# Expert rows sorted in DRAM, loaded by plain DMAs and turned on VectorE instead of TensorE

## Chip, cores and metric

The kernel runs on one core of a Trainium2 chip. The metric is device time in microseconds (us); lower is better.

## The reference, cut to what matters

```python
# x (8 batches, 8 heads, 512, 64), state (8, 8, 32, 64)
a  = softmax(scale * x @ state.T);  xread = a @ state        # 512 rows a batch
a2 = softmax(scale * state @ x.T);  sread = a2 @ x           # 32 rows a batch
x  = concat([xread, sread])                                  # 4608 tokens x 512
h  = x @ w_in                                                # dense layer, 2048 wide
x  = (h * clip(h + 3, 0, 6) / 6) @ w_out
e  = argmax(x @ w_gate)                                      # 8 experts, one for each token
out[mask] = gate_w * eom * (relu(x[mask] @ w1[e]) @ w2[e])   # expert layer, 1024 wide
```

## The kernel before

**Dense part.** Eight batches go through attention and the dense layer, 16 steps (`ft`) each; the last segment (`NB`) holds the 256 `sread` tokens of all batches together. Precision is kept by splitting each float32 operand into a high and a low part (ScalarE makes the high one by a cast, VectorE the low one by a subtraction) and by three matmuls for each product.

**Routing.** When a segment has ended, `routed` copies the layer's output to `x2`, feature by token. `write_rows` turns it into token rows (VectorE transposes of 32x32 blocks, L539) and SyncE (SP) writes these to the DRAM tensor `xd` in pieces of 512 bytes. `logits`, `turn_logits`, `choose`, `ranks` and `place` find each token's expert and its place in that expert's list; `scatter` then writes token number and weight of 128 tokens to the DRAM table `tab` at that place, one indirect DMA on GpSimd (POOL) for each tile of 128 tokens (L642).

**Expert part.** It goes in slots, in the order of `ORDER`. 16 big slots take 256 places of one expert's list each; a pair takes twice 64 places of two experts, and three pairs run here (slots 5, 10 and 18 counted from 0). For a slot `gather` reads 128 ids and weights for each half from `tab` (L868) and then the rows named there from `xd` (L874), all on POOL. `turn` then makes them feature by token: four 128x128 TensorE transposes for each 128 rows into PSUM (L889), an evacuation by ScalarE that is also the high part (L893, or L896 for a pair), and the low part from PSUM on VectorE (L894). In a big slot `gemm1` (L937, 12 matmuls a step) and `gemm2e` (L953, L956, L957, six a step, one step behind) run over 8 steps; each step needs two splits of weights (L932 and L933, L942 and L943) and one of `h` (L946, L947). `finish` scales the result and scatters it to `out` on POOL (L971). The turn of slot s+1 stands in step 4 of slot s.

**What sets the order.** The work is listed in program order, and a scheduler places each engine's instructions; every engine and every DMA queue then takes its own in order. SP issues the loads of weights (L861), two buffers of 4.2 MB for the big slots and two for the pairs, the weights of an expert being loaded only if its buffer does not hold them already. The places of the first nine big slots come from `lists1`, made in step 5 of the last dense segment; those of the rest from `lists2`, in slot 1, when the 256 `sread` tokens are placed too. The tile tag `xr` has two buffers, for `write_rows`, for the first gathered rows and for `y`; the tag `x2T` has one, for `x2` and for the scratch of the lists.

Of the kernel before, what the change touches and what calls it, by code (L numbers as in the profile page):

```python
# [19 lines left out]
DM, DF = 512, 2048  # L20
# [3 lines left out]
CAP = NT  # L24
# [22 lines left out]
def cat_consts():  # L47
# [17 lines left out]
    parts["part"] = p  # L65
    parts["high"] = p >= 64
    parts["part64"] = p % 64 + TR
# [13 lines left out]
def tile_kernel(  # L81
# [36 lines left out]
    flat = tab.rearrange("a (b o) -> (a b) o", o=2)  # L118
# [385 lines left out]
    placed = []  # L504
# [9 lines left out]
    def routed(po, n, tile0, part=None):  # L514
# [4 lines left out]
        if n == 512:  # L519
            x2.append(mp.tile([128, 2, n], F32, tag="xr", name="x2b", bufs=2) if tile0 == 28 else  # L520
                      ap.tile([128, 2, n], F32, tag="x2b", name="x2b", bufs=1))
        r.x2 = [t[:, k, :] for t in x2 for k in range(1024 // n)]
        r.made = []
# [113 lines left out]

    def scatter(r, behind=()):

        new = []  # L640
        for t in range(r.nt):
            i = G.indirect_dma_start(flat, bass.IndirectOffsetOnAxis(ap=r.dsti[:, t:t + 1], axis=0),  # L642
                                     toku[:, r.tile0 + t, :], None).ins
            for d in behind:
                tc.add_manual_dep(i, d.name, DEP, reason="rows are written first")
            for o in new:
                tc.declare_no_dep(i, o, reason="places are distinct")
            after(i, placed)
            new.append(i)
        placed[:] = new  # L650

    def route(r):
# [5 lines left out]
        if r.n > 256:  # L658
            write_rows(r, 1)
        yield  # L660
# [3 lines left out]
        place(r)  # L664
        scatter(r)
        yield
# [103 lines left out]
    def weights_regs(es, n, tag):  # L770


        regs = one("regs" + tag, 2 * n, mybir.dt.int32)
        V.tensor_copy(regs[:, :n], es)
        V.memset(regs[:, n:n + 2], 1)
        V.tensor_tensor(regs[:, n + 2:], es[:, 2:], es[:, :n - 2], op=ALU.not_equal)
# [3 lines left out]
    def list256(k, n, pos, tag, used):  # L780
# [11 lines left out]
        idu = one("idu" + tag, n, U32)  # L792
        V.tensor_scalar(idu, bases, 0.5, C("part"), op0=ALU.mult, op1=ALU.add)
        return idu, weights_regs(es, n, tag)
# [8 lines left out]
    def lists2():  # L803
# [9 lines left out]
        idm, regm = list256(2 * NE, NM, "posm", "m", took)  # L813
# [18 lines left out]
        b0, b1 = [bases.rearrange("p (j two) -> p two j", two=2)[:, i, :] for i in range(2)]  # L832
        V.tensor_tensor(b1, b1, b0, op=ALU.subtract)
        V.scalar_tensor_tensor(b1, b1, C("high"), b0, op0=ALU.mult, op1=ALU.add)
        idu = one("idu2", NP, U32)
        V.tensor_scalar(idu, b1, C("part64"), None, op0=ALU.add)
        regu = one("regsu", 2 * NU, mybir.dt.int32)
        V.tensor_copy(regu[:, :NU], es2)
        V.tensor_copy(regu[:, NU:], ok)
        used = one("used", 1, mybir.dt.int32)  # L840
        V.tensor_copy(used, total)
        return {"m": (idm, regm), "p": (idu, regu), "used": used}
# [22 lines left out]
    def gather(n, table, idx, rows):  # L865

        ids = cp.tile([128, 4], U32, tag="ids", name="ids", bufs=6)
        i = G.indirect_dma_start(ids[:, :2 * n], None, table, bass.IndirectOffsetOnAxis(ap=idx, axis=0)).ins  # L868
        after(i, placed)
        xg = []  # L870
        both = None if qa else mp.tile([128, 2, DM], F32, tag="xr", name="xg0", bufs=2)
        for t in range(n):
            x = qa["p"].tile([128, DM + 8], F32, tag="xg", name="xg", bufs=4)[:, :DM] if qa else both[:, t, :]
            G.indirect_dma_start(x, None, rows, bass.IndirectOffsetOnAxis(ap=ids[:, 2 * t:2 * t + 1], axis=0))  # L874
            xg.append(x)
        return ids, xg

    def turn(xg):

        n = len(xg)  # L880
        if n == 2:
# [461 lines left out]
```

## Time and profile before

| | |
|---|---|
| device time, median of 3 runs | 1118.22 us (1117.49 to 1118.74) |
| profiled execution, its own device time | 1119.56 us |
| its span, first to last instruction | 1117.8 us |
| granted TensorE clock, mean | 0.997 |
| TensorE busy | 1087.9 us |
| VectorE / ScalarE / GpSimd busy | 699.5 / 556.8 / 126.2 us |
| DMA moved | 128.47 MB |

The span is that of the one profiled execution; its device time is 1.76 us more than its span and 1.34 us above the median of the runs. The dense part lasts from the start to about 688 us of the span, the expert part from there to the end. A row of the chain of work gives the time from the start, the length and what it is; a row of the lines gives count, busy time and mean of one.

### The profile page before, as it was taken

The page shows a single profiled execution, that of the slowest core. Times are in us where ns is not written, and L with a number is a line of the kernel's source. Part 1 is how long each engine was busy: PE and PEld are TensorE (multiplying, and loading weights), DVE is VectorE, ACT ScalarE, POOL GpSimd, SP SyncE. Part 2 cuts the span into 40 slices and gives each one's busy share as a digit, 9 for nine tenths or more (in the row PEclk, how much of TensorE's full clock was granted, in tenths as well). Part 3 has the DMA queues.
Part 4 walks back from the last instruction along what each step waited for, and adds up shares of the span by engine and source line. Part 5 has one row for each costly group of instructions (what it writes and reads, how often), then busy time and mean ns, then how long its engine had stood idle before and what let it go on. Part 6 is the DMA issues. An engine that isn't in the chain of part 4 may idle for free.

```text
span 1117.8 us, 18409 instructions
## 1 busy us (share of the span) xinstructions
PE 1087.9 (97%) x6904; PEld 863.0 (77%) x6904; DVE 699.5 (63%) x1456; ACT 556.8 (50%) x1061; POOL 126.2 (11%) x137
## 2 busy tenths in 40 slices
PE   4899999999999999999999999999999999999997
PEld 2557776777777777777777899999869987999994
DVE  7997867755746747556555476966446645666651
ACT  4768834433434434334343345666545644666551
POOL 0000000110010010100100122331122122121101
PEclk9999999999999999999999999999999999999999
DMA  7647140411202103110010048195195769812300
GB/s 230 208 120 260 48 113 19 135 41 38 76 3 72 45 1 77 41 28 13 1 38 1 1 113 304 53 341 192 49 312 176 246 208 332 320 58 96 142 19 30
DMA packets 55007, 128.47 MB, mean 115 GB/s; under 512 B 7280, under 2 KB 25968, under 8 KB 54896
## 3 DMA queue, kind: packets, MB, share of 16 engines
q1 hardware_dynamic: 47616, 108.80, 29.8%
q0 software_dynamic: 7296, 18.43, 4.8%
q8 instruction: 56, 0.92, 0.4%
q14 instruction: 39, 0.32, 0.1%
HBM read 137.13 MB, written 19.71 MB: 140 GB/s over the span
## 4 chain that ended last, share of the span: by engine, by line
PE 93%; DVE 3%; DMA 1%; issue 1%; ACT 1%; POOL 0%; POOLq 0%; SPq 0%; DVEq 0%; ACTq 0%
PE h L460 16%; PE h L937 16%; PE o L499 11%; PE o L500 11%; PE o L501 11%; PE o L953 5%; PE o L957 5%; PE o L956 5%; PE misc L227 3%; PE h L474 2%; PE h L904 1%; PE misc L889 1%; PE o L923 1%; PE misc L553 1%; PE misc L391 1%
## 5 line engine op out<-in xcount | busy, mean ns | idle before, releaser
L500 PE MATMUL o<-gh,wo 128*128 128x512 f32 x512 | 200.5, 392 | 0.9 <-DVE wo L725 0.9
L499 PE MATMUL o<-gh,wo 128*128 128x512 f32 x512 | 199.3, 393 | 1.7 <-ACT wo L724 1.7
L501 PE MATMUL o<-gl,wo 128*128 128x512 f32 x512 | 199.9, 390 | 0.0
L490 DVE SCALAR_TENSOR_TENSOR g<-r,h 128x512 f32<-128x512 f32 x128 | 87.5, 684 | 121.2 <-ACT r L489 120.6
L489 ACT ACTIVATE r<-h 128x512 f32<-128x512 f32 x128 | 76.7, 599 | 167.6 <-PE h L460 167.5
L943 DVE TENSOR_TENSOR vl<-w2s,vh 128x512 fp32r<-128x512 f32 x128 | 89.2, 698 | 105.7 <-ACT vh L942 99.2
L942 ACT CAST vh<-w2s 128x512 fp32r<-128x512 f32 x128 | 79.3, 620 | 101.3 <-PE o L957 97.8
L491 ACT CAST gh<-g 128x512 fp32r<-128x512 f32 x128 | 79.3, 620 | 76.8 <-DVE g L490 76.0
L499 PEld LDWEIGHTS o<-gh,wo 128*128 128x128 f32 x512 | 95.9, 188 | 28.0 <-issue 4.4
L492 DVE TENSOR_TENSOR gl<-g,gh 128x512 fp32r<-128x512 f32 x128 | 88.3, 690 | 46.2 <-ACT gh L491 44.8
L500 PEld LDWEIGHTS o<-gh,wo 128*128 128x128 f32 x512 | 96.3, 188 | 23.9 <-issue 2.1
L501 PEld LDWEIGHTS o<-gl,wo 128*128 128x128 f32 x512 | 96.3, 188 | 20.4
L460 PE MATMUL h<-ah,sh 128*128 128x512 f32 x256 | 106.7, 418 | 4.3 <-ACT sh L447 2.6
L933 DVE TENSOR_TENSOR wl<-w1s,wh 128x512 fp32r<-128x512 f32 x128 | 88.4, 691 | 30.1 <-ACT wh L932 24.3
L642 POOL DMA_INDIRECT tab<-toku,ldsti x34 | 33.8, 995 | 648.6 <-DVE ldsti L636 414.2
L460 PE MATMUL h<-al,sh 128*128 128x512 f32 x256 | 102.6, 401 | 0.3 <-DVE al L291 0.3
L460 PE MATMUL h<-ah,sl 128*128 128x512 f32 x256 | 101.1, 396 | 0.1
L957 PE MATMUL o<-vh,hl 128*128 128x512 f32 x256 | 100.3, 392 | 0.0
L956 PE MATMUL o<-vl,hh 128*128 128x512 f32 x256 | 100.1, 391 | 0.0
L932 ACT CAST wh<-w1s 128x512 fp32r<-128x512 f32 x128 | 79.5, 622 | 35.5 <-PE h L937 31.5
L937 PEld LDWEIGHTS h<-xh,wh 128*128 128x128 f32 x512 | 76.5, 188 | 11.7 <-issue 2.0
L937 PE MATMUL h<-xh,wh 128*128 128x256 f32 x512 | 82.8, 283 | 0.8 <-ACT xh L893 0.8
(225 smaller groups left out, 1815.6 us busy)
## 6 DMA issues: line engine op xcount, KB each, us to landing
w1s<-w SPq DMA_DIRECT2D x88, 512.0 KB
w2s<-w SPq DMA_DIRECT2D x88, 512.0 KB
xd<-xr SPq DMA_DIRECT2D x68, 128.0 KB
xT<-xT SPq DMA_DIRECT2D x16, 512.0 KB
wi<-w_in SPq DMA_DIRECT2D x16, 512.0 KB
wraw<-w_out SPq DMA_DIRECT2D x16, 512.0 KB
xq<-xq SPq DMA_DIRECT2D x16, 512.0 KB
half<-xp SPq DMA_DIRECT2D x4, 256.0 KB
```

The costliest lines, as they stand in the source:

```text
L460: T.matmul(ps, w[:, o:o + 128], a[:, e, :], start=(n == 0), stop=(n == 5))
L490: V.scalar_tensor_tensor(g6, r, 6.0, ps, op0=ALU.min, op1=ALU.mult)
L492: V.tensor_tensor(gl, g6, gh.bitcast(F32), op=ALU.subtract)
L499: T.matmul(po[k][:, :n], woh[ft][:, s], gh, start=first, stop=False)
L500: T.matmul(po[k][:, :n], wol[ft][:, s], gh, start=False, stop=False)
L501: T.matmul(po[k][:, :n], woh[ft][:, s], gl, start=False, stop=last)
L932: S.copy(wh, a)
L933: V.tensor_tensor(wl, a, wh.bitcast(F32), op=ALU.subtract)
L937: T.matmul(ps, w[:, k, :], x[:, k, :], start=(m == 0), stop=(m == 11))
L943: V.tensor_tensor(vl, c, vh.bitcast(F32), op=ALU.subtract)
L956: T.matmul(py[t], hh[:, sl], vl, start=False, stop=False)
L957: T.matmul(py[t], hl[:, sl], vh, start=False, stop=(ft == 7))
```

## The change

Routing also sorts the rows themselves. A new DRAM tensor `xs` has a place for each place of the lists. `read_rows` reads the rows that `write_rows` has put in `xd` back into SBUF, token by partition, and `sort_rows` scatters them, whole rows of 2 KB, to their places in `xs`, one indirect DMA on POOL for each 128 tokens, two in step 11 of a segment's timetable and two in step 12; the scatter to `tab` moves to step 13 and behind them. After the last 256 tokens `zero_tails` writes 64 rows of zeros behind each expert's last row (four indirect DMAs).

An expert slot then loads its places of `xs` by plain DMAs on SP: `load_rows` reads the first place from a register, issues four pieces (a quarter of the features each, 128 floats of 256 rows, to 32 partitions), and a fifth DMA for ids and weights (`own`, from `tab`). `turn` no longer uses TensorE or PSUM: VectorE turns the pieces in 32x32 blocks, four instructions of 128x256 for a big slot (four of 128x128 for a pair), between SBUF tiles; ScalarE's cast and VectorE's subtraction then read SBUF, in two halves. The pair has no copy left. The lists give bases in place of indices, and `w1` is laid out on the host so that its rows fit the order of the features. `turn(s+1)` and the load for slot s+3 now stand in step 3 of slot s (step 4 of a pair); before, the gather for slot s+2 stood in step 1. In the last step but one of a slot, `hl` may not come ahead of the turned rows.

```diff
-    xd = tc.dram_tile([NT + 128, DM], F32, name="xd")
-    tab = tc.dram_tile([NTAB // 2, 4], U32, name="tab")
+    xd = tc.dram_tile([NT, DM], F32, name="xd")
+    xs = tc.dram_tile([NTAB, DM], F32, name="xs")
+    tab = tc.dram_tile([NTAB, 2], U32, name="tab")
...
+    def read_rows(r, c):
+        nt = min(2, r.nt - 2 * c)
+        r0 = 128 * r.tile0 + 256 * c
+        t = mp.tile([128, 2, DM], F32, tag="xr", name="xt", bufs=2)[:, :nt, :]
+        D.dma_start(t, xd[r0:r0 + 128 * nt, :].rearrange("(t p) n -> p t n", p=128))
+        r.rows.extend(t[:, k, :] for k in range(nt))
+
+    def sort_rows(r, t0, t1, behind=()):
...
+            i = G.indirect_dma_start(xs, bass.IndirectOffsetOnAxis(ap=r.dsti[:, t:t + 1], axis=0), r.rows[t], None).ins
...
     def scatter(r, behind=()):
...
+            tc.add_manual_dep(i, put[-1].name, LATER, reason="rows are wanted first")
...
     def route(r):
...
+        read_rows(r, 0)
+        if r.n > 256:
+            read_rows(r, 1)
         yield
         choose(r)
         ranks(r)
         yield
         place(r)
+        sort_rows(r, 0, r.nt)
         scatter(r)
+        if r.n == 256:
+            zero_tails()
...
-    def gather(n, table, idx, rows):
...
-            G.indirect_dma_start(x, None, rows, bass.IndirectOffsetOnAxis(ap=ids[:, 2 * t:2 * t + 1], axis=0))
+    def load_rows(bases, n):
+        xg = qa["p"].tile([128, 8, 128], F32, tag="xg", name="xg", bufs=2) if qa else \
+            mp.tile([128, 8, 128], F32, tag="xr", name="xg0", bufs=2)
+        own = cp.tile([128, 2, 2], U32, tag="own", name="own", bufs=5)
+        a = n // 32
+        for j, reg in enumerate(bases):
+            base = D.value_load(reg, min_val=0, max_val=NTAB - n)
+            for g in range(4):
+                i = D.dma_start(xg[32 * g:32 * g + 32, a * j:a * j + a, :],
+                                xs[bass.ds(base, n), 128 * g:128 * g + 128].rearrange("(a u) c -> u a c", u=32)).ins
+                after(i, put)
...
-                T.transpose(ps[:, 128 * k:128 * k + 128], xg[t][:, 128 * k:128 * k + 128], ident)
...
-                S.copy(xh[:, :, s], ps3)
-                V.tensor_tensor(xl[:, :, s], ps3, xh[:, :, s].bitcast(F32), op=ALU.subtract)
+        x = mp.tile([128, 4, 256], F32, tag="x2T", name="xt", bufs=1) if got_first else \
+            mp.tile([128, 4, 256], F32, tag="xr", name="xt0", bufs=2)
+        for c in range(2):
+            s = slice(2 * c, 2 * c + 2)
+            for k in range(2 * c, 2 * c + 2):
+                V.transpose(x[:, k, :], V_in[:, :, k, :])
+            S.copy(xh[:, s], x[:, s])
+            i = V.tensor_tensor(xl[:, s], x[:, s], xh[:, s].bitcast(F32), op=ALU.subtract)
...
+        if ft == 6:
+            tc.add_manual_dep(i.ins, last_turned[0].name, LATER, reason="the next rows first")
...
             for t in ws[1][0] + ws[1][1]:
-                G.tensor_copy(t[0:1, 0, 0:1].bitcast(U32), got[0][0][0:1, 0:1])
+                G.tensor_copy(t[0:1, 0, 0:1], got[0][1][0:1, 0, 0:1])
             fetch_weights(1)
-    fetch_rows(1)
...
+    fetch_rows(1)
+    fetch_rows(2)
...
-            if ft == 1 and s + 2 < first:
-                fetch_rows(s + 2)
-            if ft == 4 and s + 1 < first:
-                turned[s + 1] = turn(got[s + 1][1])
+            if ft == 3:
+                turn_next(s)
```

## Rows read from the trace of the kernel before

**Rows 1.** Page: busy time of engines, DMA share in 40 slices of the span.

```profile
PE 1087.9 (97%) x6904; PEld 863.0 (77%) x6904; DVE 699.5 (63%) x1456; ACT 556.8 (50%) x1061; POOL 126.2 (11%) x137
DMA  7647140411202103110010048195195769812300
```

**Rows 2.** Page: the chain that ended last, by line.

```profile
PE h L460 16%; PE h L937 16%; PE o L499 11%; PE o L500 11%; PE o L501 11%; PE o L953 5%; PE o L957 5%; PE o L956 5%; PE misc L227 3%; PE h L474 2%; PE h L904 1%; PE misc L889 1%; PE o L923 1%; PE misc L553 1%; PE misc L391 1%
```

**Rows 3.** Chain in order of time: start, us, what; slots 0 and 1, last pair's turn.

```profile
704.93 1.40 PE h L937 x12
...
727.24 0.87 PE misc L889 x8
728.12 1.42 PE h L937 x12
...
1085.09 0.44 PE misc L889 x4
```

**Rows 4.** Chain in order of time, from the dense part into slot 0.

```profile
688.07 0.14 PE o L501
...
688.23 0.62 ACT wh L932
688.85 0.98 ACT xh L893 x2
...
689.87 0.74 PE h L937 x4
```

**Rows 5.** Lines of TensorE and VectorE: count, busy us, mean ns, idle before.

```profile
L889 PE MATMUL misc<-ident,xg 128*128 128x128 f32 x140 | 18.5, 273 | 0.0
L539 DVE STREAM_TRANSPOSE xr<-x2b 128x256 f32<-128x256 f32 x32 | 11.8, 407 | 0.0
L894 DVE TENSOR_TENSOR xl<-misc,xh 128x512 fp32r<-128x512 f32 x32 | 20.5, 680 | 0.8 <-issue 0.8
L630 DVE TENSOR_TENSOR lpos<-misc,carry 128x8 f32<-128x8 f32 x34 | 5.6, 165 | 1.2
```

**Rows 6.** Windows, slots 0 to 2: us; busy of PE, PEld, DVE, ACT, POOL; clock, DMA, GB/s.

```profile
690.00:713.30 23.30, 23.26 (x160) 20.58 (x161) 21.31 (x81) 13.04 (x28) 5.51 (x5) 1.00 0.14 32
713.30:736.50 23.20, 23.20 (x155) 21.09 (x154) 20.15 (x66) 14.33 (x28) 7.83 (x7) 1.00 0.61 218
736.50:759.70 23.20, 23.20 (x154) 21.10 (x154) 14.82 (x26) 14.24 (x29) 5.38 (x5) 1.00 0.89 343
```

**Rows 7.** Timeline of VectorE at the turn in slot 3.

```profile
774.95 1.28 DVE L894 TENSOR_TENSOR xl<-misc,xh 128x512 fp32r<-128x512 f32 x2
776.15 0.68 DVE L933 TENSOR_TENSOR wl<-w1s,wh 128x512 fp32r<-128x512 f32 x1
```

**Rows 8.** Chain in order of time, the step of slot 3 behind that turn.

```profile
777.25 1.40 PE h L937 x12
```

**Rows 9.** Windows: two bursts of row writes in 512-byte pieces, a stretch of weight loads.

```profile
645.00:648.00 3.00, 3.00 (x27) 2.96 (x27) 2.17 (x6) 1.20 (x4) 0.00 (x0) 1.00 0.85 173
657.00:660.00 3.00, 3.00 (x28) 3.00 (x27) 2.00 (x10) 0.91 (x2) 0.96 (x1) 1.00 0.79 138
672.00:690.00 18.00, 17.19 (x145) 16.95 (x145) 9.82 (x20) 9.48 (x21) 6.58 (x14) 1.00 1.02 402
```

**Rows 10.** Timeline of POOL, scatters to the table.

```profile
654.17 0.96 POOL L642 DMA_INDIRECT tab<-toku,ldsti  x1 [0.30 <-issue]
655.43 1.12 POOL L642 DMA_INDIRECT tab<-toku,ldsti  x1 [0.30 <-issue]
...
703.05 1.41 POOL L642 DMA_INDIRECT tab<-toku,ldsti  x1 [23.10 <-DVE scr L766]
```

**Rows 11.** Timeline of SP's DMA issues, weights of slot 0 and of the first pair.

```profile
663.08 2.11 SPq L861 DMA_DIRECT2D w1s<-w  x4
...
724.15 2.16 SPq L861 DMA_DIRECT2D w1s<-w  x4
```

**Rows 12.** Chain in order of time, landing of rows scattered to `out`.

```profile
1099.16 2.77 DMA out<-y,ids
```

More of the change, by code (lines that the diff above doesn't have):

```diff
@@ L636, in place @@
         V.tensor_copy(r.dsti, dst)
+    def read_rows(r, c):
[5 more added lines that the diff above has]
+    def sort_rows(r, t0, t1, behind=()):
+        if t0 == 0:
+            r.sorted = []
+        for t in range(t0, t1):
+            i = G.indirect_dma_start(xs, bass.IndirectOffsetOnAxis(ap=r.dsti[:, t:t + 1], axis=0), r.rows[t], None).ins
+            for d in behind:
+                tc.add_manual_dep(i, d.name, DEP, reason="in its time")
+            for o in r.sorted:
+                tc.declare_no_dep(i, o, reason="places are distinct")
+            after(i, put)
+            r.sorted.append(i)
+        if t1 == r.nt:
+            put[:] = r.sorted
     def scatter(r, behind=()):
@@ L791, in list256 @@
         V.scalar_tensor_tensor(bases, C(pos), 256.0, bases, op0=ALU.mult, op1=ALU.add)
-        idu = one("idu" + tag, n, U32)
-        V.tensor_scalar(idu, bases, 0.5, C("part"), op0=ALU.mult, op1=ALU.add)
-        return idu, weights_regs(es, n, tag)
+        return weights_regs(es, bases, n, tag)
     def lists1():
@@ L831, in lists2 @@
         V.scalar_tensor_tensor(bases, bases, -float(TR), ok, op0=ALU.add, op1=ALU.mult)
[L832 to L837, printed above, removed]
+        regu = one("regsu", 3 * NU, mybir.dt.int32)
         V.tensor_copy(regu[:, :NU], es2)
-        V.tensor_copy(regu[:, NU:], ok)
+        V.tensor_copy(regu[:, NU:2 * NU], ok)
+        V.tensor_scalar(regu[:, 2 * NU:], bases, float(TR), None, op0=ALU.add)
         used = one("used", 1, mybir.dt.int32)
         V.tensor_copy(used, total)
-        return {"m": (idm, regm), "p": (idu, regu), "used": used}
+        return {"m": regm, "p": regu, "used": used}
     ws = {}
@@ new lines, in zero_tails @@
+    def zero_tails():
+        z = mp.tile([128, DM], F32, tag="xr", name="zeros", bufs=2)
+        G.memset(z, 0.0)
+        pair = carry.rearrange("p (j two) -> p two j", two=2)
+        ends, tails = one("ends", NE // 2), one("tails", NE // 2, U32)
+        V.tensor_tensor(ends, pair[:, 1, :], pair[:, 0, :], op=ALU.subtract)
+        V.scalar_tensor_tensor(ends, ends, C("half"), pair[:, 0, :], op0=ALU.mult, op1=ALU.add)
+        V.tensor_scalar(tails, ends, C("part64"), None, op0=ALU.add)
+        new = []
+        for j in range(NE // 2):
+            i = G.indirect_dma_start(xs, bass.IndirectOffsetOnAxis(ap=tails[:, j:j + 1], axis=0), z, None).ins
+            for o in new:
+                tc.declare_no_dep(i, o, reason="places are distinct")
+            after(i, put)
+            new.append(i)
+        put.extend(new)
@@ L1233, in bank, with turn_next @@
         return psum(f"o{(banks[0] - 1) % 4}")
+    def turn_next(s):
+        if s + 1 < first:
+            turned[s + 1] = turn(got[s + 1][1], 1 if ORDER[s + 1][0] == 'p' else 2)
+        if s + 3 < first:
+            fetch_rows(s + 3)
     def slot(s):
@@ L1238, in slot @@
             if ft == 0 and s not in turned:
[L1239 removed]
+                turned[s] = turn(got[s][1], 1 if ORDER[s][0] == 'p' else 2)
             xh, xl = turned[s]
@@ L1262, in pair @@
         if s not in turned:
-            turned[s] = turn(got[s][1])
+            turned[s] = turn(got[s][1], 1 if ORDER[s][0] == 'p' else 2)
         x, _ = turned.pop(s)
@@ L1280, in pair @@
                 hT.append(pair_turn(h[1]))
-            if ft == 4 and s + 1 < first:
-                turned[s + 1] = turn(got[s + 1][1])
+            if ft == 4:
+                turn_next(s)
             pair2(py, ft, hT[ft // 4])
```

108 lines of the change are left out of this document (53 added, 55 removed).

## The prediction

> **What bounds the kernel now.** I read the page first: TensorE is busy 97% of the span, the other compute engines 63% and less, DMA in bursts [rows 1]. Then the chain that ended last, by line: matmuls nearly throughout, and among them the transposes of L889, which do no arithmetic that the reference asks for, with 1% [rows 2]. A share of busy time alone would not say that removing work from TensorE shortens the span; the chain in order of time does. From the turn in slot 0 to that in slot 1 there are eight steps, and they go from 704.93 to 727.24, 2.79 us a step, with no wait between; then come eight transposes for 0.87 us, and the next step follows at 728.12 [rows 3]. The transposes thus stand in line with the matmuls, and what they take is taken off if nothing else comes to fill it. The windows say what could: in slots 0 and 1 VectorE is busy 21.31 us of 23.30 and 20.15 of 23.20, for there it also places the last tokens and makes the second list; from slot 2 on it is 14.82 of 23.20. The granted clock is 1.00 in all three, the upper of its two levels, 2.4 GHz [rows 6].
>
> **The change part by part.**
>
> *Transposes leave TensorE.* There are 140 [rows 5]: 16 big slots of 8 and three pairs of 4. The first big turn stands apart (below). The other 15 give back 15 x 0.87 = 13.05 us, the pairs 3 x 0.44 = 1.32 us [rows 3].
>
> *The first turn.* Its transposes run behind the last matmul of the dense part, which ends at 688.07 + 0.14 = 688.21; then the chain goes through ScalarE (a cast of weights, then the two evacuations `xh`), and the first expert matmul starts at 689.87 [rows 4]. That is 1.66 us of waiting for a turn that could not start while TensorE had other work. After the change this turn needs only the loaded rows, VectorE and ScalarE, and can lie beside the dense part's last steps. I take all 1.66 us; the lower bound is nothing, if the rows come late or VectorE turns them only after the dense part's own evacuations.
>
> *Turns on VectorE.* A big slot gets four instructions of 128x256. The nearest row is the same instruction on the same tile size in `write_rows`, 0.41 us (407 ns) [rows 5], so 1.64 us a slot. The two subtractions stay, 0.68 us each from PSUM [rows 5] and 0.68 from SBUF [rows 7], ScalarE's casts too (0.49 us each for `xh` in the chain against 0.62 for one from SBUF [rows 4]; ScalarE is the engine with more room, so nothing). In a regular slot VectorE then has 14.82 + 1.64 = 16.5 us in a slot of 22.3, which is room. What matters is the lump: 1.64 + 2 x 0.68 = 3.0 us if all comes in one piece. Before, the piece was 1.28 us, and the split `wl` queued behind it ended at 776.15 + 0.68 = 776.83 [rows 7]. Of the step that starts at 777.25 only the last third needs `wl`, two thirds of 1.40 us later, at 778.18 [rows 8]. So 1.35 us of slack were left, and a lump longer by 1.72 us would be 0.37 us late. It need not be one piece: VectorE has gaps in every step, and the only order imposed is that all be done before `hl` of step 6, three steps after it is listed. I take nothing for regular slots; the bound is 0.37 us in each of 14 of them, 5.2 us.
>
> *Slots 0 and 1.* Here VectorE has little room: slot 0 would hold 21.31 + 1.64 + 0.5 (three small operations of `zero_tails`, each 0.165 as the nearest small one [rows 5]) = 23.45 us in 23.30 - 0.87 = 22.43 us. The lists lose and gain operations about equally. Slot 1 has 20.15 + 1.64 = 21.79 in 22.33. Slot 0 is thus 1.0 us over. Part of that work is small operations for lists that nobody waits for at once, and it can slide into slot 1, even slot 2. Against this, slot 1's `hl` of step 6 stands behind slot 2's turn, and that turn shares the single `x2T` buffer with the list's scratch, so it comes after `lists2`. Between nothing (all slides) and 6.0 us (both turns' 3.0 us exposed) I take 1.5 us: the excess and half a microsecond of order.
>
> *Rows through DRAM once more.* In the dense part 17 read-backs go to SP, 34 scatters of rows to POOL. An indirect issue takes 655.43 - 654.17 = 1.26 us of POOL [rows 10], so 43 us more there, on an engine that is busy 11%, and the DMA engines have room in the middle of the dense part [rows 1]. What is behind them: the table scatters on POOL, which nobody needs before the expert part, and on SP the next segment's loads, behind a read-back that waits for writes issued two steps before. The `xr` buffers stay held until the rows are scattered, and the next `write_rows` on VectorE wants them a few steps later. I take nothing.
>
> *The load of the first rows* is where that chain is tight. The last batch's second burst of row writes ends at 660 [rows 9]. Read-back and landing, by the nearest row (2.77 us for scattered rows [rows 12]), end at 663; four scatters of 1.26 us at 668; they land at 671. SP issues slot 0's weights from 663.08 [rows 11]; 4.2 MB at 402 GB/s [rows 9] is 10.4 us, until 673.5. The pieces queue behind that: 0.52 MB at 173 GB/s, the rate of a burst of 512-byte pieces [rows 9], is 3.0 us, until 676.5. A lump of 3.0 us and a cast of 0.62 make it 680; TensorE wants it at 688.2. So 8 us of slack, and cost nothing; slot 1's weights now wait for the landed rows, and have until slot 1's start at 713.
>
> *Later loads.* Five DMAs a slot move from POOL to SP. A load is listed two slots ahead of its use, some 44 us, and takes 3.0 us of transfer. What is behind it on SP are weights. The tightest wait is that of slot 3's rows, for the last tokens' scatters: POOL starts its tables at 703.05 [rows 10]; two row scatters, two table scatters and four of zeros are 8 x 1.26 = 10.1 us, with a landing 716. The first pair's weights are issued at 724.15 [rows 11], so SP is free again before. On POOL two `out` scatters a slot stay and three gathers go. Nothing for both.
>
> **The sum.** 13.05 + 1.32 + 1.66 = 16.03 us off, 1.5 us on: 14.5 us. The profiled execution took 1119.56 us (span 1117.8 and 1.76 around it), so 1105.0 in its own terms; it was 1.34 us above the median of 1118.22, and against that the forecast is **1103.7 us**. With no cost in slots 0 and 1 it would be 1102.2; with 6.0 us there and nothing for the first turn, 1109.9.
>
> **The rivals.**
>
> *A lump in every slot.* The turn comes in one piece, 0.37 us late in 14 slots: 1103.7 + 5.2 = 1108.9. For it: instructions that become ready together are readily placed together, as the two subtractions are [rows 7]. Against: the gaps in each step.
>
> *First rows late.* The chain to slot 0 is longer than I add up by 16 us, twice the slack, since six transfers follow one another; TensorE idles 8 us: 1111.7. Against: each link has a row.
>
> *VectorE sets the pace* (the other side). If the splits have no real slack, the 1.64 us of every big turn comes on the path: from the 1102.2 of no cost, 15 x 1.64 = 24.6 us more give 1126.8. It decides from the point where two thirds of those 1.64 us show: 16.03 / 15 = 1.07 us a slot eats all the gain. For it: eight transposes cost TensorE 0.87 us [rows 3], the same work costs VectorE 1.64, nearly twice. Against: 5.9 us a slot of idle VectorE from slot 2 on, and 1.35 us of slack behind the old piece. The Trainium skill, "VectorE: DVE Perf Modes", Rules for kernel authors, speaks for this rival: a 128x128 transpose belongs on TensorE where PSUM will do as its destination. The rows agree that TensorE is the cheaper engine for it, but TensorE is also the one that the others wait for; by that rule the time would be this rival's.
>
> *SP blocks weights.* A load of rows that waits for its buffer holds up the weights behind it. A slot's weights take 10.4 us of 22.3, so a wait must exceed 11.9 us before a matmul is late; 2 us over in ten slots would give 1123.7. Against: rows wait for a turn listed just ahead of them.
>
> *The gain is not there.* Something else paces a step, and 2.79 us becomes longer as the transposes go: about 1118. Against: twelve matmuls in 1.40 us, end to end [rows 3].
>
> **How the numbers follow.** The forecast has 0.64, the lump 0.15, late rows 0.07, VectorE's pace 0.05, SP 0.04, no gain 0.05. The range from 1100.5 (the sum without costs, less 1.7 us for a start that falls out otherwise) to 1112 holds the forecast, the lump and half of the late rows, about 0.8. Its own range is 1101 to 1107. A change of 0.2%, 2.2 us, is about what a measurement of this kernel can tell. Faster: forecast, lump, late rows and a part of SP and of the no-gain case, 0.89; same: 0.04; slower: 0.07.
>
> **What would show it.** In the trace after, L889 is gone from TensorE; eight steps of a slot take 22.3 us from turn to turn; VectorE's new transposes take 0.41 us; the first expert matmul starts within 0.3 us of the last dense one; in slots 0 and 1 TensorE idles 1 to 2 us in all, waiting for VectorE. Idle time of TensorE before `wl` or `hl` in every slot shows the lump or VectorE's pace; a gap at 688 with a DMA as releaser shows late rows; one before a weight cast on ScalarE shows SP. Wrong would be above all what I have at nothing: the order on VectorE and on SP, which the scheduler draws up anew.

## The result, and the profile after

The changed kernel takes 1131.13 us (median of 4 runs, 1126.66 to 1133.26) against 1118.48 for the kernel before beside it: ratio 1.0109 (95% interval 1.0077 to 1.0141). It is slower by 1.1%, clear of its interval; the forecast was 1103.7.

The page of the changed kernel, busy time of engines and DMA share, beside [rows 1]:

```profile
PE 1078.8 (96%) x6764; PEld 852.6 (76%) x6764; DVE 719.4 (64%) x1533; ACT 554.5 (49%) x1058; POOL 114.8 (10%) x122
DMA  7648051722213114221130189387395679912300
```

TensorE has 140 instructions fewer, as forecast, and is busy 9.1 us less in a span that is 10.8 us longer (1128.6 us). So it waits. Its waits from 180 to 1120 us, after (what waited, releaser: us, times, longest):

```profile
PE h L988 <- ACT wh L983: 9.9, 4, 3.6
PE misc L226 <- ACT e L353: 2.0, 1, 2.0
PE o L500 <- DVE gl L491: 1.6, 1, 1.6
PE h L459 <- ACT sh L446: 0.7, 1, 0.7
PE misc L375 <- DVE sl L447: 0.3, 1, 0.3
PE o L1010 <- DVE hl L998: 0.2, 1, 0.2
```

and of the kernel before, in its expert part (the 0.7 us for `sh`, in the dense part, it has too):

```profile
PE h L937 <- ACT xh L893: 0.8, 1, 0.8
```

The one wait of before, at the first slot, is gone. In its place are four waits of expert matmuls for a cast of weights, `wh`, and three new waits in the dense part for tiles of ScalarE and VectorE. The third loss is at the end, in two rows of POOL's queue: its last semaphore instruction, and the drains (count: shortest, median, longest in ns):

```profile
L1364 POOLq INC_SWDGE_SEM  x1: 2326/2326/2326, 1116.7 to 1116.7; - x1
L1401 POOLq DRAIN  x3: 40/107/8805, 1119.0 to 1128.4; - x3
```

In the kernel before the semaphore instruction takes 0.515 us and the longest drain 1.455:

```profile
L1300 POOLq INC_SWDGE_SEM  x1: 515/515/515, 1115.0 to 1115.0; - x1
L1338 POOLq DRAIN  x3: 40/107/1455, 1115.5 to 1117.5; - x3
```

Against the forecast (span 1117.8 - 14.5 = 1103.3) 25.3 us are missing. The starts of two rows in both traces, the last dense matmul and the last `y`, divide them. Before, then after:

```profile
687.90 0.28 PE L501 MATMUL o<-ghl,wo 128*128 128x256 f32 x1
1111.10 0.69 ACT L970 ACTIVATE y<-o,ids 128x512 f32<-128x512 f32 x1 [7.01 <-PE o L923]
```

```profile
690.57 0.28 PE L500 MATMUL o<-ghl,wo 128*128 128x256 f32 x1
1114.95 0.69 ACT L1023 ACTIVATE y<-o,own 128x512 f32<-128x512 f32 x1 [7.01 <-PE o L974]
```

| | before | after | after, less the forecast |
|---|---|---|---|
| last dense matmul starts | 687.90 | 690.57 | +2.67 |
| from there to the last `y` (ScalarE) | 423.20 | 424.38 | +1.18 where -14.5 was forecast: 15.68 |
| last `y` to the end of the span | 6.70 | 13.65 | +6.95 |

The 688.07 of [rows 4] is where the chain's piece of that matmul begins, not its start.

### The profile page after: what moved, and what is told of

It is laid out like the page before. It is cut to its first block, busy times and chain, and to the rows that moved or that the text cites. A ratio compares the mean times of both kernels' runs of the same rounds, so it can differ in the third digit from the quotient of the medians.

```text
span 1128.6 us, 18662 instructions
## 1 busy us (share of the span) xinstructions
PE 1078.8 (96%) x6764; PEld 852.6 (76%) x6764; DVE 719.4 (64%) x1533; ACT 554.5 (49%) x1058; POOL 114.8 (10%) x122
## 5 line engine op out<-in xcount | busy, mean ns | idle before, releaser
L649 POOL DMA_INDIRECT xs<-xt,ldsti x34 | 36.4, 1070 | 575.7 <-DVE ldsti L634 344.7
```

## The experiments

Each run is beside runs of the kernel before, on the same chip. "Pieces" are the rows or runs that a transfer moves, 128 for an indirect DMA.

**The turn alone.** The kernel before with the turn on VectorE, and what that needs: slot 1's rows are fetched a little later, and one dense tile lies elsewhere. POOL still gathers whole rows, so after the 32x32 turns the features do not lie as the rows of `w1` do. This kernel leaves out what would bring them there; it shows what the turn costs in time and is no version to use.

```diff
-                T.transpose(ps[:, 128 * k:128 * k + 128], xg[t][:, 128 * k:128 * k + 128], ident)
+                V.transpose(x[:, k, :], V_in[:, :, k, :])
```

> Edit: the kernel before, with only the turn moved to VectorE (gathers from DRAM stay on POOL; the second slot's rows are fetched after the dense part, into the expert pool). The block transposes alone don't finish a turn of whole gathered rows, so the experts' outputs are not the reference's; all instructions have the shapes of the changed kernel. Theory 'the turn's gain is real': 15 turns at 0.87 us and 3 at 0.44 us off TensorE, less some VectorE stalls in slots 0 and 1: 1103 to 1106 us, big slots 22.3 us. Theory 'VectorE sets the pace': 1115 us or more, TensorE gaps ended by VectorE in many slots. Theory 'the gaps come with the turn': gaps of 2 us and more at slots 2, 8 and 13 here too, 1112 us or more.

It took 1115.36 us, ratio 0.9974 (0.9965 to 0.9984). A slot takes 22.3 us, and none of the four waits for `wh` is there, so they do not come with the turn. But one wait stands at the border of the two parts. TensorE's largest wait, and the row of VectorE that explains it:

```profile
PE h L474 <- DVE xt L895: 8.3, 1, 8.3
```

```profile
676.83 0.77 DVE L895 STREAM_TRANSPOSE xt<-xg 128x256 f32<-128x256 f32 x2 [12.09 <-DMA xg<-xd,ids]
```

The first turn stands in VectorE's order ahead of the dense part's last splits, and waits there 12.09 us for gathered rows. The splits behind it are late, and TensorE with them. Nothing but its data ties the turn to a place in that order. The next run ties it:

```diff
+    turned[0] = turn(got[0][1], marks[-1:])   # behind the dense part's last squared relu
```

> The kernel before with only the turn of the experts' rows on VectorE (gather kept, so the rows turned are as in the run with the turn alone), and the first turn's transposes ordered behind the dense part's last squared relu, so that VectorE cannot wait for gathered rows ahead of dense work. Theory, that the forecast's gains on TensorE are real and only their price elsewhere was missed: no gap of TensorE over 1 us near 678, 1104 to 1107 us. Rival, that the first turn comes late wherever it stands: a gap of 3 us or more at the first slot, 1110 us or more.

1103.73 us, ratio 0.9868 (0.9851 to 0.9884). TensorE's waits from 60 us on, and its windows of the whole expert part (us, busy of PE, PEld, DVE, ACT, POOL; clock, DMA share, GB/s):

```profile
PE h L460 <- ACT sh L447: 0.7, 1, 0.7
PE o L960 <- DVE hl L950: 0.4, 1, 0.4
```

```profile
690.00:1094.00 404.00, 403.56 (x2605) 343.51 (x2603) 268.52 (x577) 229.48 (x452) 87.81 (x81) 1.00 0.51 179
```

The expert part, from the last dense matmul (685.97) to the last `y` (1094.40), is 408.43 us against 423.20: 14.8 us shorter, where I had forecast 14.5. The theory holds: the positive terms are real. They are 1.3 us short of the 16.03 without any cost, of which 0.4 us is the wait for `hl`. The profiled span is 16.7 us shorter in all; the other 1.9 us lie in the dense part, which the sum leaves alone.

**Routing alone.** The kernel before with read-backs, sorted rows, zeros and the later table scatters, and its own gather and turn (slot 1's rows and the dense tile are moved as in the turn alone).

```diff
+        read_rows(r, 0)
...
+        sort_rows(r, 0, r.nt)
         scatter(r)
+        if r.n == 256:
+            zero_tails()
```

> Edit: the kernel before, with only the routing's part of the change added (rows read back, scattered into expert order, tails zeroed); the experts still gather from the unsorted rows and TensorE still turns them. Theory 'routing has its own price': gaps of 3 to 4 us between 200 and 224 us as in the changed kernel and up to 3 us with no releaser near 670 us, 1122 to 1127 us. Theory 'only SP's order costs': within 1.5 us of the kernel before. For the tail: 'bookkeeping' says 6.7 us from the last scaling to the end (skipped bodies as in the kernel before), 'row scatters' says over 11 us.

1130.17 us, ratio 1.0106 (1.009 to 1.0123): 11.7 us for what I had put at nothing. Two of its waits:

```profile
PE misc L230 <- ACT e L357: 2.0, 1, 2.0
PE o L504 <- DVE gl L495: 1.2, 1, 1.2
```

They are the changed kernel's own. In that kernel, VectorE and POOL just before:

```profile
202.70 0.77 DVE L537 STREAM_TRANSPOSE xr<-x2T 128x256 f32<-128x256 f32 x2 [6.58 <-issue]
```

```profile
191.61 1.12 POOL L649 DMA_INDIRECT xs<-xt,ldsti  x1 [190.29 <-ACT r L488]
```

The first routed rows are held in `xr` until POOL's scatters (from 191.61 on) have read them; the transposes of the next `write_rows` want the buffer, wait 6.58 us, and hold up VectorE's splits behind them. The row names no releaser; the next run shows it. TensorE then idles 1.59, 2.02 and 0.30 us at 204, 215 and 220. Of routing alone's profiled execution, 10.6 us longer than before, 3.6 us are these waits, 4.2 us the end (last `y` to end 10.9 us), and 2.9 us a dense part that runs slower without waits (last dense matmul at 694.34), for a reason that stays open. Its expert part is as long as before's.

**Rows sorted a step earlier.** The changed kernel with those first rows scattered in the half segment's last step, before the next `write_rows`.

```diff
-            if n == 3 and ft < f0 + 2:
-                sort_rows(unplaced, 2 * (ft - f0), 2 * (ft - f0) + 2, marks[-1:])
+            7: [..., lambda: sort_rows(r, 0, 4)],
```

> Edit: the changed kernel, with the four row scatters of the batch that is routed in the half segment issued in that segment's last step, in place of the first two steps of the next one. Theory 'held buffers' (the read-back buffers are held until these scatters land, and the next row write waits for them): the 6.58 us wait of VectorE at 195 to 203 us and the 3.9 us of TensorE gaps at 200 to 224 us go; all later times come 3 to 4 us earlier, 1126 to 1128.5 us. Theory 'traffic' (the routing's extra megabytes collide with the loads of x wherever they are put): gaps of the same sum elsewhere before 260 us, and the time stays within 1 us of the changed kernel.

The waits at 204 to 220 are gone, which shows the cause. The time is 1139.35 (1.0184) all the same: idle stretches with no releaser came in, 1.59 us near 185 and 2.69 near 668, and four more waits for ScalarE and VectorE from 722 to 748, 3.8 us. Only the first lies near the edit; far from it, too, the scheduler places instructions otherwise than before.

**What moves the slots.** At slots 2, 3, 8 and 13 TensorE waits 3.60, 1.41, 2.44 and 2.44 us. Slot 8 of the changed kernel, ScalarE, then TensorE:

```profile
873.04 1.26 ACT L1023 ACTIVATE y<-o,own 128x512 f32<-128x512 f32 x2 [1.91 <-PE o L1010]
874.20 1.13 ACT L927 CAST xh<-xt 128x512 fp32r<-128x512 f32 x2
875.22 1.66 ACT L983 CAST wh<-w1s 128x512 fp32r<-128x512 f32 x3
```

```profile
875.90 0.74 PE L988 MATMUL h<-xh,wh 128*128 128x256 f32 x4 [2.44 <-ACT wh L983]
```

Nothing here waits for a DMA. ScalarE evicts the old slot (1.26 us), then casts the rows of the slot **after** this one (1.13), and only then the first weights that this slot needs. At slot 13 it is the same; at slot 3 only the evictions stand ahead. At slot 2 a real wait is added: the cast of slot 3's rows, ahead of `wh` here too, waits for their turn, and the turn for the rows.

```profile
739.34 1.42 DVE L926 STREAM_TRANSPOSE xt<-xg 128x256 f32<-128x256 f32 x4 [2.80 <-DMA w1s<-w]
```

The releaser shown is a weight load, but SP's rows tell more. They are its last read of a place of the second list, slot 3's rows (from the timeline), and the first four issues for slot 2's weights (count: shortest, median, longest in ns).

```profile
L895 SPq TENSOR_LOAD <-regsu x1: 275/275/275, 734.0 to 734.0; - x1
734.96 1.90 SPq L897 DMA_DIRECT2D xg<-xs  x4
L884 SPq DMA_DIRECT2D w1s<-w x4: 73/76/99, 737.8 to 739.2; - x4
```

Slot 3's place is in the first list, but SP reads places of the second list into registers ahead of it, and VectorE makes these late, among the turns: the first pair's experts at 731.42, where the kernel before has them at 723.17 (`regsu`). So the rows go out at 734.96. The weight issues behind them move next to nothing (76 ns each where a load's issue takes some 340, and 28 GB/s from 738 to 740): slot 2's expert is in its buffer already.

What follows a gap is a second cost. The windows behind the one at slot 8:

```profile
872.00:876.00 4.00, 1.55 (x8) 0.98 (x6) 2.08 (x5) 2.96 (x6) 1.69 (x2) 1.00 0.70 235
876.00:880.00 4.00, 4.00 (x22) 4.00 (x23) 2.97 (x6) 1.89 (x4) 0.37 (x1) 0.58 0.86 257
880.00:884.00 4.00, 4.00 (x32) 3.92 (x32) 2.88 (x6) 3.39 (x7) 0.00 (x0) 1.00 0.57 172
```

TensorE is busy again from 876 to 880 and gets 22 matmuls done, 32 in the next 4 us: the granted clock is 0.58, nearly the lower level, 1.2 GHz. In the 12 us from about the end of each of the three longer gaps the clock is 0.86; behind the fourth gap, 1.41 us long, it is 1.00 (767 to 779).

```profile
741.00:753.00 12.00, 11.01 (x64) 10.23 (x65) 8.43 (x15) 7.87 (x16) 0.19 (x1) 0.86 0.94 305
875.00:887.00 12.00, 11.10 (x66) 10.48 (x67) 8.94 (x16) 7.40 (x16) 1.10 (x1) 0.86 0.66 203
985.00:997.00 12.00, 11.58 (x66) 10.76 (x67) 8.61 (x16) 7.40 (x15) 0.89 (x1) 0.86 0.39 89
```

By my estimate that is 12 x 0.14 = 1.7 us each and 5.0 together, beside 10.1 us of idle. Two runs ask where this order comes from. First, the turn held behind the slot's own fourth step, nothing else changed:

```diff
                 i = V.transpose(x[:, k, :], V_in[:, :, k, :])
+                for d in behind:
+                    tc.add_manual_dep(i.ins, d.name, LATER, reason="this slot's own steps first")
```

> Edit: the changed kernel, with the four block transposes of the next rows ordered behind VectorE's last subtraction of the slot's own fourth step (an order alone, no wait). Theory 'order' (the casts of the next rows stand ahead of the slot's own weight casts on ScalarE at the starts of slots 2, 8 and 13): the TensorE gaps of 3.60, 2.44 and 2.44 us there fall to 1.5 us or less each, and with the clock drops behind them the end comes 6 to 11 us earlier than the changed kernel's, 1120 to 1125 us. Theory 'late weights' (the weights themselves land late because the row loads stand before them on SP): the gaps stay, now ended by the weights' DMAs, and the time stays at 1128 to 1133 us.

1130.25 us (1.0106). The expert matmuls' waits for `wh` shrink from 9.9 to 5.7:

```profile
PE h L990 <- ACT wh L985: 5.7, 4, 1.4
PE h L473 <- issue: 2.9, 3, 1.0
```

Each is now 1.41 to 1.45 us, the two evictions alone. Slot 3's rows go out about as late as in the changed kernel (3.7 us ahead of the end of slot 1's matmuls, there 3.4), so what the gaps lost was the order on ScalarE. From slot 1's `y` to the last one it is 368.7 us instead of 376.9, 8.2 us less. But the time stays, against what was expected: slots 0 and 1, where VectorE is nearly full, lose 3.2 us (from the last dense matmul to slot 1's `y`), 2.7 of them in two waits near the held turns,

```profile
725.89 0.73 PE L1009 MATMUL o<-vh,hh 128*128 128x512 f32 x2 [1.06 <-ACT hh L999]
745.96 0.72 PE L1013 MATMUL o<-vh,hl 128*128 128x512 f32 x2 [1.63 <-DVE hl L1000]
```

and the dense part ends 6.5 us later, 2.9 of them with no releaser, as above. Second, the loads of rows, ids and registers on POOL's queue in place of SP's:

```diff
-                i = D.dma_start(xg[32 * g:32 * g + 32, a * j:a * j + a, :],
+                i = G.dma_start(xg[32 * g:32 * g + 32, a * j:a * j + a, :],
```

> Edit: the changed kernel, with the loads of rows and token numbers (and the register loads for them) issued from POOL's queue in place of SP's. Theory 'SP order' (both kinds, late weights and an order planned around late weights, come from the rows standing in SP's queue): no TensorE gap over 0.5 us at any slot start, all big slots at 22.3 us, the last scaling of the last pair at 1099 to 1103 us, the time 1108 to 1117 us depending on the kernel's tail (7 to 14 us). Theory 'VectorE' (the transposes on VectorE make the gaps): gaps of over 2 us stay at three or four slot starts and the time stays over 1125 us. Theory 'traffic' (the 512-byte pieces slow the weights' transfers): gaps stay, ended by weight DMAs.

1122.32 us, ratio 1.0041 (1.0029 to 1.0054), 8.8 us less than the changed kernel. None of the four gaps is left and a slot takes 22.3 us; one new wait came, for the same reason on another engine (TensorE, then VectorE, whose transposes wait for rows ahead of the split `wl`):

```profile
PE h L988 <- DVE wl L984: 4.5, 1, 4.5
```

```profile
768.64 0.45 DVE L926 STREAM_TRANSPOSE xt<-xg 128x256 f32<-128x256 f32 x1 [4.83 <-DMA xg<-xs]
```

Between the profiled spans of the changed kernel and this one (9.5 us less) the expert part is 10.8 us shorter and the end 2.5, and the dense part 3.8 longer. This shows that the four gaps go when rows, ids and their register reads leave SP. That they come by way of the scheduler, which reckons SP's loads and so the weights late and fills ScalarE with the next slot's rows, is argued from the order in the rows above, not shown by itself. The Trainium skill, "DMA: Bandwidth & Descriptors", Issuing engine by pattern, gives simple loads to SyncE, as the generally faster path. Here the measurement says otherwise: the queue that has the weights was the wrong one for them.

**The end.** Six runs go after the 7.0 us. First come four. Tail pairs' ids on POOL (were they bookkeeping that runs on?), zeros made by VectorE, no conditional tail, and the kernel before with one more POOL memset:

```diff
+                i = W.dma_start(own[64 * j:64 * j + 64, 0, :], tab[bass.ds(b2, n), :]).ins   # W = G
...
-        G.memset(z, 0.0)
+        V.memset(z, 0.0)
...
-    for s in range(first, len(ORDER)):
...
+            tc.add_manual_dep(G.memset(one("zz", 8), 0.0).ins, placed[-1].name, LATER, reason="after the last scatter")
```

> Edit: the changed kernel, with the token numbers of the six skipped tail pairs (the code under the conditions, not run here) loaded from POOL's queue, so that a skipped body holds three POOL transfers as in the kernel before. Nothing that is run before the last scaling changes. Theory 'bookkeeping of skipped transfers' (in the changed kernel the count that POOL makes good for skipped transfers leaves out the semaphore of the last scatter, so it starts while that scatter is under way, and POOL's drain behind it takes 8.8 us): the drain goes back to 1.5 us, from the last scaling to the end 6.7 us in place of 13.7, the time 6 to 8 us below the changed kernel's. Theory 'row scatters' (the drain grows because POOL scattered whole rows earlier): drain still 8.8 us, time unchanged.

> Edit: the changed kernel, with the tile of zeros for the experts' tails set by VectorE in place of POOL; nothing else. Theory 'memset' (POOL's one computing instruction late in the kernel leaves POOL slow in what it does last: in runs without it the last semaphore instruction and drain took 0.5 and 1.5 us, in runs with it 1.3 to 2.3 and 4.4 to 8.8): 0.5 and 1.5 us, from the last scaling to the end 6.7 us, the time 7 to 9 us below the changed kernel's. Theory 'row scatters' (they, not the memset, are what the slow runs share): drain still 8.8 us, time unchanged.

> Edit: the changed kernel without the six conditional tail pairs, which are skipped on this input anyway; what is left out is only needed for other inputs. Without them POOL has no semaphores to make good at the end. Theory 'bookkeeping is what is slow': no drain over 2 us, from the last scaling to the end under 7 us. Theory 'memset' and theory 'row scatters': the drain itself stays long, 4 us or more.

> Edit: the kernel before, with one memset of a 128 x 8 tile on POOL behind the last scatter of token numbers; nothing reads it. Theory 'memset': the drain at the end grows from 1.5 to 4 us or more, the time by 3 us or more, 1121 us and up. Theory 'row scatters': drain 1.5 us, 1118 us.

1133.86, 1128.09, 1128.31 and 1122.84 us. The first two keep their drain of 8.805 us to the nanosecond, the third, which has no such semaphore instruction any more, has 10.008, the fourth has before's 1.455: bookkeeping and memset both fell. (The first's end is even 2.7 us longer: POOL now waits 2.2 us for its last scatter ahead of the semaphore instruction.) What else is different is how much POOL's transfers move: 34 + 34 + 35 + 4 = 107 indirect DMAs in the changed kernel, 123 in the one before. So the changed kernel got 16 small loads on POOL, 128 pieces each, to make up before's count exactly; and the kernel before got 12 loads of 512 pieces on top:

```diff
+                for k in range(16):
+                    i = G.dma_start(spare[:, 2 * k:2 * k + 2], fill[128 * k:128 * k + 128, :]).ins
```

> Edit: the changed kernel with 16 more small loads on POOL's queue in its sixth slot (128 pieces of 8 bytes each, into an unused tile; nothing reads them). Theory 'count' (POOL puts off some work for each piece that its transfers move and does it at the end, unless a count between 13,696 and 15,744 pieces, the changed kernel's and the kernel before's, makes it do it on the way): with 15,744 pieces POOL's last semaphore instruction and drain take 0.5 and 1.5 us in place of 2.3 and 8.8, and from the last scaling to the end it is 6 to 7 us in place of 13.7; time 6 to 8 us below the changed kernel's. Theory 'row scatters' (they leave the work behind, whatever the count): 2.3 and 8.8 us, time unchanged.

> Edit: the kernel before with 12 more loads on POOL's queue in four slots (512 pieces of 8 bytes each; nothing reads them): 21,888 pieces. Theory 'count', with a limit near 15,400: 6,500 pieces are left for the end, and by the runs so far (1.97 us with some 400 left, 5.8 with some 5,300, 11.1 with 13,696) the last semaphore instruction and the drain take 5.5 to 7 us together in place of 1.97, the time 3.5 to 5 us above the kernel before. Theory 'row scatters': 1.97 us, time unchanged (the loads hide on POOL).

Drains of the first and of the second:

```profile
L1405 POOLq DRAIN  x3: 46/103/2167, 1131.1 to 1133.8; - x3
```

```profile
L1343 POOLq DRAIN  x3: 46/103/3745, 1115.3 to 1119.6; - x3
```

More transfers made the changed kernel's end **shorter**: from the last `y` to the end 5.3 us instead of 13.7. And they made before's longer, 9.6 instead of 6.7 (1121.62 us, ratio 1.0033). The first run's time is no lower, 1133.91, for 7.1 us of other waits, and the clock behind them, came in with the new order: 3.1 us with no releaser near 670, and 4.0 at 727. Last semaphore instruction and longest drain together, by the pieces that POOL's transfers move (counted from the kernels):

| pieces | kernels | us |
|---|---|---|
| 13,696 | the changed kernel and four of its variants | 11.13 |
| 15,744 | before, the turn alone, tied or not, one more memset | 1.97 |
| 15,744 | the changed kernel with 16 loads | 2.71 |
| 20,608; 21,888 | routing alone; before with 12 loads | 5.85; 4.83 |
| 31,616; 34,816 | fifth; fourth version below | 3.52; 5.25 |
| 36,096 | rows on POOL, first to third version | 5.66 to 5.76 |
| 48,384 | sixth version | 4.23 |

The edit of these two runs is nothing but more transfers, and the end moved with them, in both directions. So row scatters do not set it by themselves. It goes with the count, but not evenly: it falls and rises again, and the same count gave 1.97 and 2.71. That is how work of a queue that is cleared in rounds would look, but no size of a round fits all these rows (20,608 pieces take longer than 21,888). Which rule it is, and whether pieces are its measure, stays open.

**Versions put together.** The first has rows on POOL, the turn held, the tail pairs' rows on SP; the second adds the rows sorted a step earlier.

```diff
-    def load_rows(bases, n):
+    def load_rows(bases, n, Q=G):
...
-        fetch_rows(s)
+        fetch_rows(s, D)
         pair(s)
```

> Edit: the changed kernel with rows loaded from POOL's queue in the slots, the turn ordered behind the slot's own fourth step, and in the skipped tail rows by SP and token numbers by POOL. Theory 'order and queue': the 4.48 us gap at 770 us of the run with POOL's queue alone (VectorE held by the next rows' transposes) goes, all slots at 22.3 us, tail 6.7 us; what is left of the loss is the dense part's 3.9 us and up to 3 us near 670 us: 1108 to 1113 us. Theory 'rows on POOL are too late by themselves': a gap of over 3 us stays near 770 us, now ended by the rows' own transfers, 1114 us or more.

> Edit: as the run before it (rows on POOL, turn held, tail mended), and the batch routed in the half segment scatters its rows in that segment's last step. Theory 'held buffers': the gaps between 200 and 224 us go against some 1.6 us near 186 us, 2 to 3 us earlier than the run before it, 1105 to 1111 us. Theory 'scatters starve TensorE's instructions wherever they stand': as much lost near 186 us and 670 us as gained, within 1 us of the run before it.

1116.46 (0.9985, 0.9975 to 0.9994), and **1112.46** us (1112.39 to 1112.62), ratio 0.9947 (0.993 to 0.9964): the fastest version here that loads the sorted rows, ahead of both kernels. It has one wait of size, at 683.71, and the longer end:

```profile
PE o L500 <- DVE ghl L491: 3.4, 1, 3.4
PE h L459 <- ACT sh L446: 0.7, 1, 0.7
```

```profile
690.00:1100.00 410.00, 409.99 (x2650) 348.51 (x2648) 271.26 (x590) 233.41 (x460) 104.00 (x142) 1.00 0.57 187
```

In its expert part TensorE does not idle, and from the last dense matmul (692.33) to the last `y` (1100.35) it is 408.0 us, as in the second run of the turn alone, here with rows that lie as `w1` needs them. Against that run's profiled span it is 9.7 us longer, 6.4 of them in the dense part and 3.75 at the end: the price of sorting the rows in this version. The 3.4 us are the first turn waiting for rows ahead of dense splits. Four more versions, each from the second, try to take that and the end away: the third has the zeros by VectorE (the first rows by SP, which was meant too, its edit did not bring), the fourth the first rows by SP, the fifth ids on SP and the first turn tied, the sixth the first turn tied and 24 loads of 512 pieces.

```diff
+            fetch_rows(0, D)
...
+    turned[0] = turn(got[0][1], 2, marks[-1:])
```

> Edit: as the best run so far (rows on POOL's queue, turn held behind the fourth step, half segment's rows scattered at its end, tail mended), with the zeros set by VectorE and the first slot's rows loaded by SP. Theory 'memset' takes 3 to 4 us off the tail, and SP for the first rows takes the 3.45 us gap at 684 us with its clock drop: 1103 to 1107 us. If the drain comes from the row scatters, 1107 to 1110 us. If the first rows are late on either queue, the gap stays and the time is 3 to 4 us higher.

> Edit: the best version so far (rows on POOL's queue, turn held behind the fourth step, the half segment's rows scattered at its end), with the first slot's rows and token numbers loaded by SP, which the last run's edit was meant to do and did not. Theory 'POOL brings the first rows late' (its scatters of token numbers stand before them): the 3.5 us gap at 683 us goes, with its clock drop, 4 to 5 us off: 1107 to 1110 us. Rival: the transposes of the first rows stand too early on VectorE whatever brings them: the gap stays over 2 us, 1111 to 1113 us. Theory 'count' for the tail: 34,816 pieces, with limits near 15,400 some 4,000 left: last semaphore instruction and drain 4.5 to 5.3 us together.

> Edit: the version with rows on POOL's queue, turn held behind the fourth step and the half segment's rows scattered at its end, and two more: the token numbers of the slots' rows by SP, which takes POOL's pieces from 36,096 to 31,616, and the first slot's transposes ordered behind the dense part's last multiply step on VectorE. Theory 'count' (a limit between 13,696 and 15,744 pieces, passed twice by 31,616): at most some 4,200 pieces are left, last semaphore instruction and drain 2 to 5 us together in place of 5.7. The 3.5 us gap at 683 us goes, with its clock drop. 1104 to 1109 us. Rival: SP's register loads for the token numbers bring gaps back at slots 2 and 3: 1110 us or more.

> Edit: the same with all row loads and token numbers on POOL as in the version that c4 starts from, the first slot's transposes ordered as in c4, and 24 loads of 512 pieces more on POOL that nothing reads: 48,384 pieces in place of 36,096. Theory 'count': the limit is passed three times, at most 7,300 pieces are left and near 2,200 if the limit is near 15,400: last semaphore instruction and drain 2 to 4 us together in place of 5.7, and the kernel with more transfers ends 1 to 4 us earlier than without: 1104 to 1108 us. Rival (the late loads themselves, or the row scatters, set the drain): 5.7 us or more, 1108 us or more.

1113.21, 1120.26, 1117.83 and 1116.15 us. The wait at 683 went in the last three (in the third version it stayed, 3.5 us), but idle stretches without releaser came in near 186 and 676. Two rows of TensorE in the fourth version:

```profile
675.70 0.28 PE L500 MATMUL o<-ghl,wo 128*128 128x256 f32 x1 [1.04 <-issue]
677.18 0.28 PE L499 MATMUL o<-ghl,wo 128*128 128x256 f32 x1 [1.07 <-issue]
```

## Why the prediction was wrong

**The gain was right.** A slot without a gap takes 22.3 us in the changed kernel, as forecast, and TensorE is busy in all of it:

```profile
1055.50:1077.80 22.30, 22.30 (x145) 20.23 (x145) 15.07 (x30) 13.28 (x27) 2.06 (x2) 1.00 0.07 25
```

The run with the turn tied gives the whole sum, 14.8 us.

**The first turn was right.** After the last dense matmul TensorE goes on without a wait (1.03 us of logits, which before stood behind the first expert matmuls, then the first expert matmul at 691.74). Of the 1.66 us, which I had called waiting, only 0.81 was idle time of TensorE before; the rest was the eight transposes. Both are gone.

**VectorE's price was right, and my allowance for slots 0 and 1 was not needed in the changed kernel.** Forecast 0.41 us an instruction, measured 418 ns:

```profile
L926 DVE STREAM_TRANSPOSE xt<-xg 128x256 f32<-128x256 f32 x64 | 24.1, 418 | 3.7 <-DMA w1s<-w 2.8 <-DMA own<-tab 0.9
```

No wait of 0.25 us or more stands in the changed kernel between 221 and 741 us; the 1.5 us did not come. The lump and VectorE's pace, two of the rivals, did not come either. VectorE's pace would have given 1126.8; the turn alone, tied, gave 1103.73. The Trainium skill, "VectorE: DVE Perf Modes", Rules for kernel authors, sends a 128x128 transpose to TensorE, and spoke for that rival. Here, where TensorE sets the pace, the dearer engine was the cheaper place.

**The step that failed first is "Later loads ... Nothing for both."** It cost 15.7 us between the last dense matmul and the last `y`: slots 0 and 1 were 1.5 us better than forecast, so 17.2 us of loss, of which 10.1 us are idle, an estimated 5.0 us the clock behind the three longer gaps, and 2.1 us I cannot place. I had summed when the tightest rows land (716 by my reckoning), but not that SP's reading of places into registers stands in one line with the loads of rows and weights. Slot 3's rows went out at 734.96, behind the second list, whose small operations I had let slide as ones that "nobody waits for at once": SP did. The rival "SP blocks weights" had the place, but its price was a real lateness of over 11.9 us a slot. What happened at slots 3, 8 and 13 needs no late transfer: another order on ScalarE is enough, 1.4 or 2.4 us each time. My last line named the order as the weak point; it had no price in the sum or the range.

**"The `xr` buffers stay held ... I take nothing" failed too.** The wait is 6.58 us of VectorE and 3.9 us of TensorE, once, at the first routed rows; the last dense matmul is 2.7 us later than before.

**The end was not in the sum at all.** It is 7.0 us. As many small loads as the change had taken from POOL shorten the end by 8.4 us, so fewer POOL transfers, which I had booked as pure relief ("On POOL ... three gathers go"), are what lengthened it; by what rule is open.

Together: 15.68 + 2.67 + 6.95 = 25.3 us, the miss.

## What to carry to other kernels

When a change moves loads to a queue that carries the loads of the pacing engine, price the order and not only the bytes: what is listed behind a load that waits, and what the other engines will do first meanwhile. A part that removes work from the bottleneck is best tried alone and tied by order, as here, where it gave 14.8 us that the whole change lost again. And the time from the last result to the end of the span is a term of its own; read it in both traces.

## What the runs showed of the hardware

The drain of POOL's queue at the end took 1.455 us in the kernel before, with 15,744 pieces moved, and 8.805 in the changed kernel with 13,696; 16 small loads more took it from 8.805 to 2.167. TensorE showed idle stretches of 0.3 to 1.1 us that no releaser explains, some 0.7 or 1.4 us apart, near 186 us and between 666 and 679 us, during POOL's scatters of rows or those to the table right behind them; seven of the kernels have them, eight others that scatter the same rows do not, and the cause is open. One more tile of 32 bytes a partition, with a memset on POOL, made the kernel slower by a ratio of 1.0034 (1.0021 to 1.0047) with no new wait: its first expert matmul comes at 693.16 instead of 689.87, and the 128 matmuls of one form between 300 and 600 us, that run and then before, take a mean of 398 ns in place of 394:

```profile
L460 PE MATMUL h<-al,sh 128*128 128x512 f32 x128 | 50.9, 398 | 0.0
```

```profile
L460 PE MATMUL h<-al,sh 128*128 128x512 f32 x128 | 50.5, 394 | 0.0
```

These 4 ns a matmul are a part of the 3.3 us; where the rest lies, and whether the place of the tiles is the cause, is not shown. But a few microseconds of a comparison here can come from something else than what the edit is about.
